# Loading half of batch 0's values in rows, and multiplying g into the tokens instead of the weights

## The chip, the cores and the metric

The kernel runs on one core of a Trainium2 chip. The core has five instruction queues that run side by side and wait for each other through semaphores: TensorE (PE, matrix products and turns), VectorE (DVE), ScalarE (ACT), GpSimd (POOL) and SyncE (SP). POOL and SP also issue the transfers between the chip's main memory and the core's on-chip memory. The metric is the device time of one launch in microseconds, less is better.

## The reference, cut to what matters

Two blocks follow each other. The first is attention in chunks: 4 batches, 8 heads, 768 positions, 64 values per head. Each chunk of 32 queries sees 8 memory keys, 16 keys to its left, its own 32 and 8 to its right, 64 in all.

```python
for c in range(nc):
    l_start = max(0, c_start - left_ctx)
    r_end = min(S, c_end + right_ctx)
    k_full = np.concatenate([mem_k, k[:, :, l_start:r_end]], axis=2)
    v_full = np.concatenate([mem_v, v[:, :, l_start:r_end]], axis=2)
    scores = scale * np.matmul(q_c, k_full.transpose(0, 1, 3, 2))
    a = np.exp(scores - scores.max(-1))
    a = a / (a.sum(-1) + 1e-09)
    out[:, :, c_start:c_end] = np.matmul(a, v_full)
```

The second is a normalisation and a two-layer network over the 512 features of each position, added to its input:

```python
xn = (x - mu) / np.sqrt(var + 1e-06) * g_ln
ch = np.maximum(xn @ w_ch1, 0.0) @ w_ch2
return x + ch
```

The vector `g_ln` has one factor per feature. It can be multiplied into the tokens `x - mu` or, since it runs along the rows of `w_ch1`, into that matrix. The division by the root is the same for a whole token and positive, so the kernel does it last, on the result of the second product.

## The kernel before, in words

The tokens are worked in 24 tiles of 128 positions, six to a batch. Tile t goes through these steps:

- `qk(t)`: 64 small products of queries and keys into PSUM (L316), the row maximum (`row_max`, L325, DVE), the difference (`less_max`, L328, DVE) and the exponential (`weights`, L338, ACT).
- `pt(t)`: four turns of the weights on PE (L348) and a copy.
- `val(t)`: 32 small products with the values `V` (L362), then `tokens` on DVE (sum of weights, quotient, mean; L371 to L378), and `shift`, which takes the mean off and rounds to 16 bits (`xn`; L385 on POOL, L389 on ACT).
- `turn_x(t)`: four turns on PE (L414) and a copy into `xT` (L420).
- `root(t)`: the variance on ACT (L400) and two small POOL instructions for `rstd` (L404, L408).

Two tiles are a unit u, twelve in all. `up(u, s)` for s from 0 to 7 is the first layer (L452) with its relu (L443 or L445). The second layer is `down(0, part)` (L477) for unit 0 and `down7(u, part)` (L528) for the others: seven products of blocks, from sums of the relu's results (`r_sum`, L522) and of w2's blocks (`w2_sum`, L507).

The keys and queries come in as octets of rows (`load_octets`, L111, two transfers a call) and are turned on PE into streams with blocks of 72 columns. For batches 1 to 3 two heads are first interleaved by a copy (`mix`, L246), so that one turn (L255) does the work of two (L214).

The values lie in `V[b % 2]`, 128 rows for each of 12 groups of 64 positions: the memory's rows, the rows that a group's two chunks share, and the rest. In batch 0 all values go the way of the keys: octets, turns (`turn_v`) into the stream `VT`, then per group eight turns (`v_products`, L285) and a copy into `V` (`v_copy`, L296). From batch 1 on they are loaded by head straight into rows (`load_v_head`, L120 and L125, and `load_v_ends`, L131 and L135, all issued on POOL in pieces of 64 values); the shared rows are copied inside the chip by `v_shared` (L142) and the memory's by `v_mem` (L147), both issued on SP.

The order of the work is written out by hand: straight code for units 0 and 1 (L603 to L819), then a plan of calls by unit and step (L821 to L904). Every engine runs its own part of that order and never overtakes. That holds for the issue of transfers too: a load on POOL stands in line with POOL's fills and small sums, a copy on SP in line with the stores of finished tokens. In the straight code PE is also given products of zeros (`warm`, L599) where it would have nothing to do.

In the code before, POOL multiplies g into the four quarters of w1 (`scale_w1`, L434, 16 calls) after their loads: the first two quarters before the loads of w1's third and fourth, the last two after the loads of w2.

## Time and profile before

| what | value |
|---|---|
| time, median of 3 runs (lowest, highest) | 231.99 us (231.17, 232.43) |
| the profiled execution: its time, its span | 231.75 us, 230.0 us |
| PE, DVE, ACT, POOL busy | 95%, 70%, 54%, 50% of the span |
| w2's last quarter lands | 38.23 us |
| POOL's last load of batch 1's values: issue ends, lands | 60.83 us, 62.34 us |
| `val(2)`, `val(4)`, `val(6)` start on PE | 32.92, 46.18, 69.19 us |
| up(2, 0), the first product of unit 2, starts on PE | 59.34 us |

The profile is of one execution. Its times count from the start of the span; 1.75 us of the execution's time lie around the span. PE's busy time holds the products of zeros too, so a busy PE in the first 20 us is not all useful work. A page has the busy times, the span in 40 slices, the chain of work that ended last and the costliest groups; further views list the instructions of an engine in order of time (start, duration, line, what was written and read, how often; in brackets the idle time before it and what ended it), and the busy times by stretches. The trace also has the time at which most transfers landed.

### The profile page before, as it was taken

Reading aid. Unit: us, or ns where it says so; the run is one execution under the profiler, and the core shown is the slowest. Engines: PE = TensorE matmul, PEld = TensorE weight load, DVE = VectorE, ACT = ScalarE, POOL = GpSimd, SP = SyncE. Lnnn points to the kernel's source line nnn. Section 1 sums busy time; section 2 is a strip of 40 time slices with the busy share of each in tenths; the row PEclk is TensorE's granted clock in tenths of the full one; section 3 lists DMA queues with packets and bytes.
Section 4 is the critical chain, followed back from the end, with each engine's and each line's share of the span. In section 5 each row is a group of like instructions: output and inputs, shape, how many; then the busy total and the mean of one; then the engine's idle time right before and its main releaser. Section 6 shows DMA issues by size and latency. Waiting matters only on the chain.

```text
span 230.0 us, 8554 instructions
## 1 busy us (share of the span) xinstructions
PE 218.4 (95%) x3720; PEld 190.0 (83%) x3720; DVE 162.1 (70%) x380; ACT 124.6 (54%) x237; POOL 115.4 (50%) x197
## 2 busy tenths in 40 slices
PE   7979787999999989999999999999999999999993
PEld 3546675886898979989989999999999999899982
DVE  3576654678998996796587796894784875646372
ACT  2244475888552748649645468478447265343310
POOL 7889897589965594913724946513031121220000
PEclk9999999999999999999999999999999999999999
DMA  5999999998999899963881992942102002011022
GB/s 79 188 205 205 214 215 200 187 77 55 61 155 152 149 90 111 138 87 42 149 115 51 119 154 56 106 91 67 48 3 91 3 3 91 3 48 46 1 94 93
DMA packets 43282, 23.25 MB, mean 101 GB/s; under 512 B 29884, under 2 KB 39676, under 8 KB 43172
## 3 DMA queue, kind: packets, MB, share of 16 engines
q0 software_dynamic: 38320, 14.48, 52.9%
q1 hardware_dynamic: 4924, 8.22, 12.8%
q8 instruction: 29, 0.48, 0.8%
q14 instruction: 9, 0.07, 0.1%
HBM read 29.02 MB, written 6.29 MB: 153 GB/s over the span
## 4 chain that ended last, share of the span: by engine, by line
PE 86%; DVE 6%; issue 3%; ACT 2%; POOL 1%; DVEq 0%; POOLq 0%
PE upb L452 34%; PE dnb L528 28%; PE two L362 4%; PE one L255 3%; PE dnb L477 3%; PE one L316 3%; PE one L414 2%; PE two L599 2%; PE one L348 2%; POOL raw L111 1%; DVE sub L328 1%; DVE xs L372 1%; DVE KT L227 1%; DVE nmx L325 1%; ACT rT L443 1%
## 5 line engine op out<-in xcount | busy, mean ns | idle before, releaser
L452 PE MATMUL upb<-xT,w1c 128*128 128x256 f16 x736 | 94.9, 273 | 1.6 <-issue 1.4
L452 PEld LDWEIGHTS <-w1c 128*128 128x128 f16 x736 | 77.8, 114 | 3.6 <-issue 1.5
L443 ACT ACTIVATE rT<-upb 128x512 f16<-128x512 f32 x92 | 53.5, 594 | 37.8 <-PE upb L452 34.9
L535 DVE SCALAR_TENSOR_TENSOR xs<-dnb,rstd,xs 128x256 f32<-128x256 f32 x77 | 37.0, 481 | 27.2 <-PE dnb L528 26.3
L528 PEld LDWEIGHTS <-RS 128*128 128x128 f16 x352 | 33.8, 98 | 3.7 <-issue 0.2
L338 ACT ACTIVATE P<-sub 128x512 f16<-128x512 f32 x24 | 15.2, 634 | 37.1 <-DVE sub L328 36.8
L528 PE MATMUL dnb<-T,RS 128*128 128x256 f16 x264 | 33.9, 273 | 0.0
L385 POOL TENSOR_SCALAR xn<-xs,nmean 128x512 f16<-128x512 f32 x18 | 12.7, 707 | 35.6 <-PE upb L452 20.6
L404 POOL TENSOR_SCALAR veps<-ssq 128x1 f32<-128x1 f32 x24 | 4.9, 204 | 45.9 <-ACT sq L400 45.6
L528 PEld LDWEIGHTS <-rT 128*128 128x128 f16 x264 | 25.2, 98 | 2.5
L528 PE MATMUL dnb<-w2c,rT 128*128 128x256 f16 x176 | 22.7, 272 | 0.0
L522 DVE TENSOR_TENSOR RS<-rT 128x1024 f16<-128x1024 f16 (+2 forms) x23 | 15.2, 663 | 8.9 <-ACT rT L443 8.9
L120 POOL DMA_DIRECT2D V<-in_v_dram x24 | 20.9, 871 | 1.2 <-PE dnb L528 0.7
L400 ACT ACTIVATE sq<-xs,nmean 128x512 f16<-128x512 f32 x24 | 17.3, 721 | 0.1
L372 DVE CUSTOM_DVE_ANT_1 xs<-two,rec 128x512 f32<-128x512 f32 x24 | 16.6, 691 | 0.8
L325 DVE TENSOR_REDUCE nmx<-one 128x8 f32<-128x512 f32 x22 | 15.1, 685 | 1.2 <-PE one L316 1.2
L408 POOL TENSOR_TENSOR rstd<-veps,mhalf 128x1 f32<-128x1 f32 x24 | 14.9, 621 | 2.0
L328 DVE TENSOR_TENSOR sub<-one,nmx 128x512 f32<-128x512 f32 x22 | 15.2, 692 | 0.8
L125 POOL DMA_DIRECT2D V<-in_v_dram x24 | 15.5, 647 | 0.0
L353 ACT COPY PT<-one 128x512 f16<-128x512 f16 x21 | 12.2, 586 | 5.6 <-PE one L348 5.6
L255 PEld LDWEIGHTS <-raw 96*128 96x128 f16 x192 | 10.6, 97 | 2.0 <-issue 0.8
L420 DVE COPY xT<-one 128x512 f16<-128x512 f16 x21 | 8.8, 420 | 4.5 <-PE one L414 4.1
(115 smaller groups left out, 312.2 us busy)
## 6 DMA issues: line engine op xcount, KB each, us to landing
out_dram<-xs SPq DMA_DIRECT2D x23, 256.0 KB, 2.5
raw<-in_k_dram POOLq DMA_DIRECT2D x16, 192.0 KB, 5.8
raw<-in_q_dram POOLq DMA_DIRECT2D x12, 192.0 KB, 6.3
w1c<-in_moe_w_ch_dram POOLq DMA_DIRECT2D x4, 512.0 KB, 8.8
w2c<-in_moe_w_ch_dram POOLq DMA_DIRECT2D x4, 512.0 KB, 12.5
V<-in_v_dram POOLq DMA_DIRECT2D x24, 77.0 KB, 3.7
V<-V SPq DMA_DIRECT2D x3, 360.0 KB
V<-in_v_dram POOLq DMA_DIRECT2D x24, 44.0 KB, 3.4
```

What stands on the lines that cost most here:

```text
L120: nc.gpsimd.dma_start(out=V[b % 2][72:128, 0 : NG - 1, h, 0:64], in_=dram(v, base + 16 * D, [[64, 56], [64 * 64, NG - 1], [1, 64]]),)
L125: nc.gpsimd.dma_start(out=V[b % 2][0:32, 1:NG, h, 0:64], in_=dram(v, base + 48 * D, [[64, 32], [64 * 64, NG - 1], [1, 64]]),)
L255: nc.tensor.matmul(out=pv[:, 96 * r : 96 * r + 96], lhsT=mixed[i][0:96, jj, r, :], rhs=identity[0:96, 0:96], is_transpose=True, start=True ...
L325: nc.vector.tensor_reduce(out=nmx[t % 2], in_=scores, axis=AX.X, op=ALU.max)
L328: nc.vector.tensor_tensor(out=sub[t % 2].rearrange("p (c k) -> p c k", c=8), in0=scores, in1=free(nmx[t % 2], 0, [[1, 8], [0, 64]]), op=AL ...
L338: nc.scalar.activation(out=P[t % 3], in_=sub[t % 2], func=ACTF.Exp, scale=0.125)
L372: nc.vector.tensor_tensor_reduce(out=x.rearrange("p (h d) -> p h d", h=H), in0=free(two, 0, [[128, 8], [1, 64]]), in1=free(r, 0, [[1, 8], ...
L400: nc.scalar.activation(out=sq, in_=xs[t % 9], func=ACTF.Square, bias=nmean[t % 6], scale=1.0, accum_out=ssq[i],)
L443: nc.scalar.activation(out=o, in_=i, func=ACTF.Relu)
L452: nc.tensor.matmul(out=p[:, 256 * hb : 256 * hb + 256], lhsT=free(w1c[hc // 4][:, dt, :], hc % 4, [[4, 128]]), rhs=xT[u % 3][:, dt, :], st ...
L528: nc.tensor.matmul(out=p[:, 0:256], lhsT=left[:, n, :], rhs=right(n), start=(n == 0 and not add), stop=(n == 7), skip_group_check=add,)
L535: nc.vector.scalar_tensor_tensor(out=x, in0=p[:, 0:256], scalar=rstd[t % 9], in1=x, op0=ALU.mult, op1=ALU.add,)
```

## The change

Five things are changed, all but one of them in the straight code for units 0 and 1.

1. The second half of batch 0's values is no longer loaded as octets and turned. A new function loads a group of `V` in rows, in two transfers, and groups 5 to 11 come that way, spread between the loads of w1 and w2 on POOL. Their memory rows and shared rows come by `v_mem(0, 5)` and `v_shared` on SP. Groups 0 to 4 are made as before.
2. `scale_w1` is gone. g is loaded as a row repeated on all 128 partitions (`g_row`), and `shift` multiplies it into the tokens: on DVE in one instruction for tiles 0 to 5 (they were on ACT), on POOL in two for the other 18 tiles (it was one).
3. The second keys and queries of batch 0 are interleaved like those of later batches: the keys by two copies on POOL, the queries by two on ACT, and then turned in half as many matmuls.
4. The two turns of the memory's keys and values are joined into one, and the memory rows of all batches are loaded at once and earlier.
5. The order of the code at the start is written anew. The fills of `V[1]` (`ready_v`) keep their place on POOL, between the first and the second loads of batch 1's keys and queries; ahead of them now stand all row groups. Some relus, copies and products of zeros change engine or number; 99 tiny products of zeros replace seven large ones at the very start.

```diff
+    def load_v_group(b, g):
+        lo = b * H * HS + 64 * g * D
+        rows = 56 if g < NG - 1 else 48
+        nc.gpsimd.dma_start(
+            out=V[b % 2][72 : 72 + rows, g, :, 0:64],
+            in_=dram(v, lo + 16 * D, [[64, rows], [HS, H], [1, 64]]),
+        )
+        nc.gpsimd.dma_start(
+            out=V[b % 2][0:32, g, :, 0:64],
+            in_=dram(v, lo - 16 * D, [[64, 32], [HS, H], [1, 64]]),
+        )
...
             nc.gpsimd.tensor_scalar(
-                out=xn[i], in0=x, scalar1=nmean[t % 6], scalar2=1.0, op0=ALU.add, op1=ALU.mult,
+                out=xc, in0=x, scalar1=nmean[t % 6], scalar2=1.0, op0=ALU.add, op1=ALU.mult,
             )
+            nc.gpsimd.tensor_tensor(out=xn[i], in0=xc, in1=g_row, op=ALU.mult)
         else:
-            nc.scalar.activation(
-                out=xn[i], in_=x, func=ACTF.Identity, bias=nmean[t % 6], scale=1.0,
+            nc.vector.scalar_tensor_tensor(
+                out=xn[i], in0=x, scalar=nmean[t % 6], in1=g_row, op0=ALU.add, op1=ALU.mult,
             )
...
+    nc.sync.dma_start(out=g_row, in_=dram(moe_g_ln, 0, [[0, 128], [1, 512]]))
...
     load_w1(0)
-    load_w1(1)
     load_octets(0, 1, k, 0, 48, 48)
     load_octets(1, 1, q, 0, 32, 64)
-    load_octets(2, 1, v, 0, 48, 48)
+    load_w1(1)
+    load_mem_rows(0, B)
+    load_w1(2)
+    mix(0, 1, "P", 1)
...
+    mix(1, 1, "A", 0, 128)
...
+    last_k(0, "A")
+    last_k(1, "A")
+    load_v_group(0, 5)
+    load_w1(3)
+    for g in (6, 7):
+        load_v_group(0, g)
+    v_mem(0, 5)
+    v_shared(0, 5, 8)
...
+    for c in range(2):
+        load_w2(c)
+    for g in (8, 9):
+        load_v_group(0, g)
     for c in range(2, 4):
         load_w2(c)
...
+    for g in (10, 11):
+        load_v_group(0, g)
+    v_shared(0, 8, NG)
...
-    for c in range(2, 4):
-        for dt in range(4):
-            scale_w1(c, dt, "P")
     load_octets(0, 0, k, 1, 0, 48)
     load_octets(1, 0, q, 1, 0, 48)
-    load_mem_rows(1, B)
     ready_v(1, nc.gpsimd)
     v_mem(1)
...
-    v_turn(5, "V")
...
-    val(2, "A")
+    val(2, "V")
...
     load_octets(0, 1, k, 1, 48, 48)
     load_octets(1, 1, q, 1, 48, 48)
...
-    up(1, 5, "V")
+    up(1, 5, "A")
```

## The prediction

> **What bounds the kernel now.** I read the page first: PE is busy 95% of the span, and in the 40 slices it is short of full only in the first eight. The chain that ended last says the same: 86% PE, most of it the two big products (L452, L528). So after about 45 us every microsecond is PE work in a fixed order, and a change can win or lose time only by when PE gets through the start, or by a new wait later.
>
> Next the table by stretches (engine busy times, then granted clock, DMA share, GB/s) and the page's DMA rows:
>
> ```profile
> PE   7979787999999989999999999999999999999993
> DMA  5999999998999899963881992942102002011022
> 20.00:25.00 5.00, 4.78 (x137) 3.81 (x134) 3.02 (x7) 2.59 (x4) 4.05 (x8) 1.00 1.24 206
> ...
> 35.00:40.00 5.00, 3.57 (x96) 2.73 (x94) 2.01 (x7) 2.59 (x5) 3.74 (x7) 1.00 1.19 201
> 50.00:55.00 5.00, 5.00 (x83) 3.14 (x81) 4.37 (x15) 3.81 (x9) 4.76 (x8) 1.00 0.63 42
> ```
>
> The DMA share stays above 1 (packets overlap) from 5 to 45 us: the POOL queue's transfers land one after another without a gap. It falls to 0.63 only after 50 us. So a transfer added at the start moves all that follow it.
>
> Then the order of time on POOL, on SP's queue and on PE:
>
> ```profile
> 38.78 1.14 POOL L111 DMA_DIRECT2D raw<-in_q_dram  x2 [0.83 <-DMA w2c<-in_moe_w_ch_dram]
> 40.24 0.84 POOL L120 DMA_DIRECT2D V<-in_v_dram  x1 [0.32 <-DMA raw<-in_k_dram]
> ...
> 60.26 0.57 POOL L135 DMA_DIRECT2D V<-in_v_dram  x1
> 62.31 0.79 SPq L142 DMA_DIRECT2D V<-V  x1
> 46.18 0.42 PE L362 MATMUL two<-V,PT 64*32 64x65 f16 x32
> 69.19 0.42 PE L362 MATMUL two<-V,PT 64*32 64x65 f16 x32
> ```
>
> A load on POOL waits until the eighth load before it has landed: the one at 38.78 waits for w2's last quarter, which the trace lets land at 38.23. POOL then issues all of batch 1's values, its last load at 60.26 to 60.83, landing at 62.34. Only then can SP start the copy of the shared rows (62.31), whose packets end at 67.86. The first use of those values is `val(6)` on PE at 69.19. So this chain has only 69.19 - 67.86 = 1.3 us to spare.
>
> **The change part by part.** The profiled execution took 231.75 us (span 230.0, 1.75 around it), 0.24 below the median 231.99; sums are made on 231.75.
>
> *PE, ACT, DVE at the start.* PE loses seven `v_turn` (38.85 to 39.20: 0.35 each, 2.45), two value turns (28.64 to 29.44: 0.8), half of four k/q turns (8 matmuls on L255 take 0.34 where 16 on L214 take 0.5 to 0.64: about 0.9) and one of two mem turns (half of 0.86): 4.6 us. DVE and ACT lose seven copies into V (0.41 or 0.60 each). ACT is instead held by `mix(1, 1, "A")` behind q's second half (now landing near 18), so `PT(1)` is copied about 2 us later than its 18.23; the relu of `up(1, 5)` and `up(1, 7)` (0.69 each) goes from DVE to ACT, while DVE takes the shift of tokens 0 to 5 (nearest rows 0.69 for a subtract, 0.80 for L484, against ACT's 0.72). I cost all of this at nothing: it lies ahead of `val(4)`, where the next item ends last. That cover is about five microseconds thick: from `val(2)` to `val(4)` PE had 46.18 - 32.92 = 13.3 us with 1.6 of idling and 1.4 of `v_turn` in it; with val(2) near 32, PE would now be at `val(4)` near 42.
>
> *POOL before 40 us.* It loses 16 scalings of w1 (0.68 each, 10.9 us) and two octet loads (1.2); it gains two `mix` copies 96x1024 (between 0.98, a memset of 128x1024, and 2.3, by 0.289 for 32x128 on L693; I take 1.37, two scalings' worth, the like-sized read and write), 14 row loads (0.6 to 0.7 each by the 384-row and 128-row L131, L135) and as many more slots in the wait of eight. All of it is issued ahead of the full queue, so it costs nothing there.
>
> *The transfers.* Ahead of w2's last quarter the queue loses v's second half (20.65 to 22.40 in landings: 1.75) and gains five row groups of 448 + 256 pieces. Price of a piece: V's first two loads, 616 each, landed 1.38 us after the queue's load before them (46.08 to 47.46), so 1.12 ns and 0.79 us a group. Low bound 0.83 ns (352 + 616 + 616 landing between 50.35 and 51.67), 0.59 us; high bound 1.56 ns (1936 pieces from 58.36 to 61.38, paced by POOL's issue), 1.10 us. I take 0.79, the row with the fullest queue: 3.95. The mem rows come earlier (192 pieces added 0.15 at 42.10: 0.2). g as 128 rows, 256 KB, on SP's queue beside the first k (whose second load landed at 6.64): 0.4, between 0 and 0.8 (by one 256 KB tile at 204 KB/us being 1.3, less g's old 512 small pieces). SP's copies of mem and shared rows, some 230 KB at 204 KB/us, 1.1 at most, 0 if they fit between; I take 0.7. Sum: -1.75 + 3.95 + 0.2 + 0.4 + 0.7 = +3.5, between +1.4 and +5.9. w2's last quarter lands at 41.7. The Trainium skill, DMA: Bandwidth & Descriptors, "Anatomy of one DMA", gives the moving part as bytes / 436 GB/s, 0.41 us for a group's 180 KB read; by it the sum here would be +1.6 and the time some 1.9 lower. The 1.12 ns row is the measurement, and it stands.
>
> Behind this, `val(4)` needs the copy of groups 8 to 11, which waits for group 11 (43.0): with the 1.75 us that SP's copy needed from issue to first packet (62.31 to 64.06) and about 1.3 of packets, 46.1. It was at 46.18. So PE gains nothing by then, and 23.0 us of unbroken PE work (46.18 to 69.19) follow as before.
>
> *POOL behind w2.* The second half of q for batch 1 (first set) now waits for w2's last quarter, 0.28 after it (as at 10.80 after 10.52): 42.0. From there POOL has no free time: that load 0.57, the four fills of V[1] (33.47 to 36.57: 3.1, which before lay ahead of the wait and now lie behind it), four octet loads 2.3, eight L120 7.2, eight L125 5.3, the ends 1.2, four `root` pairs 3.9: 23.6. Last issue ends at 65.6 instead of 60.83: +4.8. Before, POOL had 2.8 us of waits for ACT in this stretch; they are eaten up.
>
> *The new wait.* Less the 1.3 us to spare, `val(6)` waits until 72.7: +3.5, between +1.4 and +5.9. Behind it on PE stands everything that is left; SP's stores of tokens 0 and 1 stand behind the copy, their buffers being needed only by `val(9)` (86.42).
>
> *g in the shift.* From token 6 on POOL does a second pass per tile, 18 times. Its price is not in the trace: at least one one-input pass (0.69, L385), at most two (1.38); I take 1.0, since it reads two tiles and writes one. Time between shift and turn in before: token 6 1.02, 7 1.19, 8 0.53, 9 1.83, 22 1.54, the others 1.7 and more. Token 6 just holds. Token 7 is hit twice, since POOL puts two q loads (1.15) between the shifts: 71.63 + 1.0 + 1.15 + 0.05 + 0.69 + 1.0 = 75.5 against a turn at 75.08, 0.4. Token 8, where POOL works without a gap from 79.71: 86.52 + 1.0 - 87.05 = 0.5. Later ones are covered by the 1.5 to 2.8. Sum +0.9 (0.3 to 2.0). The row says 0.69 for one input; the Trainium skill, GPSIMD Engine Reference, "Elementwise — side-by-side cycle accounting", gives 2.6 cycles an element at 1.2 GHz for two inputs, 1.1 us here, by which this item would be 1.2. No run here shows it yet.
>
> Together 231.75 + 3.5 + 0.9 = 236.15, so **236.1 us, slower by 1.9%**. Its own range, from 1.4 + 0.3 to 5.9 + 2.0, is 233.4 to 239.6.
>
> **The rivals.** *Faster: the row groups fill holes.* If the five groups, g and SP's copies add nothing to the queue, w2's last quarter lands at 36.5, POOL's last issue ends at 36.8 + 23.6 = 60.4 and V[1] is ready at 67.4; `val(4)` is released near 41, PE reaches `val(6)` before 67.4, 1.7 less than 69.19. With the cheap second pass: 231.75 - 1.7 + 0.3 = 230.3. For: POOL lags behind the queue nowhere, and PE's 4.6 us are real. Against: a share above 1 for 40 us. It decides once all additions together stay below some 0.5 us.
>
> *Nearly even: the wait is just covered.* With every addition at its low end (+1.4), and POOL's 23.6 us of issues some 1.2 us quicker, `val(6)` moves by 0.2 and, with 0.3 to 0.9 for the shift, the time is 232.2 to 232.9. Against: POOL's loads in 53 to 61 us ran without a wait and were no quicker.
>
> *Slower by another place: the second pass is dear.* If it takes 2.5 us, all turns of odd tokens from 9 on are late by 0.7 to 0.8 (slack 1.7), eight of them 6 us, beside the wait for V[1]: 240 or more. Nothing in the trace speaks for so much.
>
> **How the numbers follow.** Main case 0.57; dear second pass or another slower cause 0.14; nearly even 0.09; faster 0.20. The time can be told from no change at about 0.5%. Slower 0.71, same 0.09, faster 0.20. The low end 230.3 is the faster rival's own time and leaves out what lies beyond it, about 0.1; the high end 239.6 is the main case's upper bound and leaves out the dear pass beyond it.
>
> **What would show it.** Right: DMA share above 1 until past 50 us; w2's last quarter landing near 41.7; PE idle before L362's successor (`val`) near 42 to 46 and again near 69 to 73, the latter ended by SP's copy; POOL without a gap from 42 to 66; one turn of tokens 7 and 8 waiting for POOL. Wrong: V[1]'s last load landing before 64, a `val(6)` that does not wait, or row groups landing in 0.5 us each.

## The result, and the profile after

The changed kernel takes 241.36 us, the median of four runs (240.01 to 242.22). Before, measured beside it, takes 232.21 us (231.17 to 232.94). The ratio is 1.039, with a 95% interval from 1.032 to 1.046: the change costs about 9 us, where the terms of the forecast added up to 4.4. Runs that lie over 1.5% above the fastest of their kernel are left out of medians, ranges and ratios below. The profiled execution of after took 242.22 us with a span of 240.5; before's span was 230.0. All places below count from the start of a span, so 10.5 us have to be found; the profiled execution is the slowest of its four, and the medians differ by 9.2. Executions of a kernel can differ by a few us here, and places by as much as 1.5: in the profiles of four kernels whose code is the same up to `val(6)` (after twice, and two experiments below that change only POOL's second pass), w2's last quarter lands at 41.28 to 42.10 and `val(6)` starts at 72.67 to 74.14. So medians and ratios decide, and places are used where they differ by more than that or lie close together in one trace.

From the page of after, PE, the granted clock and DMA in 40 slices of 6 us, then the chain that ended last by engine:

```profile
PE   6687849999986697999999999999999999999993
PEclk9999985999999999999999999999999999999999
DMA  4999999999999959595294396962201102011022
...
PE 51%; DMA 14%; DVE 11%; POOL 11%; ACT 7%; issue 6%; POOLq 0%; ACTq 0%; SPq 0%; DVEq 0%
```

Before, PE was full from the eighth slice on, but for an 8 in the fifteenth. Now it has a second hole in the 12th to 14th slices, 66 to 84 us, and a smaller one in the 16th, 90 to 96. The chain that ended last was 86% PE; now DMA, DVE, POOL and "issue" have large shares. The table by stretches (busy time of PE, of its weight load, of DVE, ACT and POOL with counts, then granted clock, DMA share, GB/s) shows the holes in the start and at `val(6)`, and the transfers that now come later:

```profile
34.00:38.00 4.00, 1.90 (x39) 1.59 (x40) 1.14 (x5) 0.59 (x1) 1.64 (x3) 0.61 1.35 213
38.00:42.00 4.00, 4.00 (x82) 2.75 (x81) 2.91 (x7) 0.60 (x1) 1.86 (x4) 0.54 1.41 183
...
50.00:55.00 5.00, 5.00 (x77) 3.46 (x75) 3.30 (x12) 4.16 (x12) 4.16 (x8) 1.00 1.23 145
69.00:74.00 5.00, 2.07 (x22) 1.71 (x19) 2.42 (x5) 2.93 (x6) 3.60 (x6) 1.00 0.86 143
```

The DMA share from 50 to 55 us is 1.23; it was 0.63. The order of time on POOL, then on SP's queue, then on PE, gives the chain behind that:

```profile
42.39 0.58 POOL L110 DMA_DIRECT2D raw<-in_q_dram  x1 [1.77 <-DMA w2c<-in_moe_w_ch_dram]
42.95 1.40 POOL L579 MEMSET V<- 128x1536 f16 x1
...
55.01 0.84 POOL L119 DMA_DIRECT2D V<-in_v_dram  x1 [0.41 <-DMA raw<-in_k_dram]
...
57.70 1.36 POOL L124 DMA_DIRECT2D V<-in_v_dram  x2 [0.69 <-issue]
...
66.74 0.53 POOL L147 DMA_DIRECT2D V<-in_v_dram  x1
68.56 0.78 SPq L154 DMA_DIRECT2D V<-V  x1
36.10 0.62 PE L370 MATMUL two<-V,PT 64*32 64x65 f16 x30 [3.27 <-DMA V<-V]
...
74.14 0.42 PE L370 MATMUL two<-V,PT 64*32 64x65 f16 x32 [3.08 <-DMA V<-V]
```

w2's last quarter landed at 42.10 (38.23 before). The q load that waits for it goes out at 42.39, the fills of `V[1]` come behind it, POOL's last value load is issued by 67.27 (60.83), the copy of the shared rows on SP at 68.56 (62.31), and `val(6)` starts at 74.14 instead of 69.19. PE would have been there at 71.06 and stands still for 3.08 us.

Where the span's 10.47 us (242.22 - 231.75) went, by PE's starts of the same step in both traces (worked out from the two orders of time on PE):

| place | us |
|---|---|
| `val(6)` starts later: 74.14 - 69.19 | 4.95 |
| turn of token 6 | 0.38 |
| a stop of PE behind `val(7)`, 78.95 to 80.84, "issue" | 2.06 |
| turn of token 8, which waits for POOL's second pass | 0.92 |
| turns of tokens 10, 11, 16 and 17 (0.40, 0.38, 0.51, 0.27) | 1.56 |
| the end, and what is below 0.2 each | 0.60 |

So 4.95 us are lost by `val(6)` and 5.52 behind it. The second sum is the surprise. The groups of after that bear on it (busy us, mean ns of one, then idle time before them and what ended it):

```profile
L396 POOL TENSOR_TENSOR xn<-xc,g_row 128x512 f16<-128x512 f32 x18 | 23.3, 1293 | 1.5
L393 POOL TENSOR_SCALAR xc<-xs,nmean 128x512 f32<-128x512 f32 x18 | 12.9, 717 | 33.9 <-PE upb L445 20.1 <-DVE nmean L386 13.6
L515 DVE TENSOR_TENSOR RS<-rT,RS 128x1024 f16<-128x1024 f16 x11 | 11.5, 1043 | 0.0
```

and the same two places in before:

```profile
L385 POOL TENSOR_SCALAR xn<-xs,nmean 128x512 f16<-128x512 f32 x18 | 12.7, 707 | 35.6 <-PE upb L452 20.6 <-DVE nmean L378 14.5 <-PE one L414 0.4
L522 DVE TENSOR_TENSOR RS<-rT,RS 128x1024 f16<-128x1024 f16 x11 | 7.5, 681 | 0.0
```

POOL's second pass takes 1293 ns. And one of the sums on VectorE, which the change does not touch, went from 681 to 1043 ns on average. It is not slower everywhere: five of the eleven take 1.45 to 1.47 us, one 0.75, the others 0.68 as before. Those five start while POOL's second pass runs. In the sixth meeting the sum starts first, at 143.17; it takes 0.75, and POOL's pass, begun at 143.46, takes 1.59. In the order of time of after, one such meeting on DVE, POOL and PE:

```profile
109.32 0.69 DVE L336 TENSOR_TENSOR sub<-one,nmx 128x512 f32<-128x512 f32 x1
109.92 1.45 DVE L515 TENSOR_TENSOR RS<-rT,RS 128x1024 f16<-128x1024 f16 x1
111.30 0.47 DVE L528 SCALAR_TENSOR_TENSOR xs<-dnb,rstd,xs 128x256 f32<-128x256 f32 x1
111.70 1.01 DVE L238 COPY KT<-one 128x192 f16<-128x192 f16 x2
109.55 1.28 POOL L396 TENSOR_TENSOR xn<-xc,g_row 128x512 f16<-128x512 f32 x1
112.75 0.38 PE L423 MATMUL one<-identity,xn 128*128 128x128 f16 x4 [0.33 <-DVE KT L238]
```

POOL's pass runs from 109.55 to 110.83. The sum starts at 109.92 and ends at 111.38, 0.55 after the pass. The subtraction just ahead of it, which reads PSUM, runs beside the same pass and keeps its 0.69. What follows on DVE is 0.78 late, and the turn of token 10 on PE waits for it.

The trace of before has one such meeting, the other way round, on DVE and POOL:

```profile
197.37 0.68 DVE L522 TENSOR_TENSOR RS<-rT,RS 128x1024 f16<-128x1024 f16 x1
197.62 0.98 POOL L385 TENSOR_SCALAR xn<-xs,nmean 128x512 f16<-128x512 f32 x1 [6.77 <-DVE nmean L378]
```

There POOL's one pass begins 0.25 into the sum, takes 0.98 where such a pass takes 0.69 elsewhere, and ends 0.56 after the sum. So in all these meetings the operation that starts second ends some 0.5 us or more after the first, and the sign of it stood in the trace that the forecast was made from.

### The profile page after: what moved, and what is told of

It is laid out like the page before. It is cut to its first block, busy times and chain, and to the rows that moved or that the text cites. A ratio compares the mean times of both kernels' runs of the same rounds, so it can differ in the third digit from the quotient of the medians.

```text
span 240.5 us, 8427 instructions
## 1 busy us (share of the span) xinstructions
PE 217.5 (90%) x3654; PEld 189.0 (79%) x3654; DVE 164.7 (68%) x372; ACT 123.6 (51%) x234; POOL 137.7 (57%) x213
## 4 chain that ended last, share of the span: by engine, by line
PE 51%; DMA 14%; DVE 11%; POOL 11%; ACT 7%; issue 6%; POOLq 0%; ACTq 0%; SPq 0%; DVEq 0%
PE upb L445 21%; PE dnb L521 18%; DMA raw<-in_k_dram 8%; DMA V<-in_v_dram 3%; PE dnb L470 3%; DMA V<-V 2%; ACT rT L436 2%; POOL V L119 2%; PE two L370 2%; DVE RS L515 2%; DVE xs L528 2%; PE one L423 2%; DVE sub L336 2%; DVE nmx L333 2%; ACT sq L409 2%
## 5 line engine op out<-in xcount | busy, mean ns | idle before, releaser
L445 PE MATMUL upb<-xT,w1c 128*128 128x256 f16 x752 | 98.4, 276 | 2.5 <-issue 1.9
L445 PEld LDWEIGHTS <-w1c 128*128 128x128 f16 x752 | 80.3, 115 | 5.3 <-issue 2.7
L436 ACT ACTIVATE rT<-upb 128x512 f16<-128x512 f32 x96 | 56.0, 596 | 42.9 <-PE upb L445 42.9
L346 ACT ACTIVATE P<-sub 128x512 f16<-128x512 f32 x24 | 15.2, 632 | 41.7 <-DVE sub L336 41.7
L393 POOL TENSOR_SCALAR xc<-xs,nmean 128x512 f32<-128x512 f32 x18 | 12.9, 717 | 33.9 <-PE upb L445 20.1
L396 POOL TENSOR_TENSOR xn<-xc,g_row 128x512 f16<-128x512 f32 x18 | 23.3, 1293 | 1.5
L370 PEld LDWEIGHTS <-PT 64*32 64x32 f16 x768 | 7.9, 95 | 13.5 <-issue 11.4
L370 PE MATMUL two<-V,PT 64*32 64x65 f16 x768 | 11.0, 195 | 8.0 <-DMA V<-V 6.4
L361 ACT COPY PT<-one 128x512 f16<-128x512 f16 x21 | 12.1, 584 | 6.8 <-PE one L356 6.8
L417 POOL TENSOR_TENSOR rstd<-veps,mhalf 128x1 f32<-128x1 f32 x24 | 14.1, 586 | 2.0
L379 DVE RECIPROCAL rec<-two 128x8 f32<-128x8 f32 x24 | 4.8, 200 | 14.1 <-PE two L370 13.9
```

The costliest lines, as they stand in the source:

```text
L346: nc.scalar.activation(out=P[t % 3], in_=sub[t % 2], func=ACTF.Exp, scale=0.125)
L370: nc.tensor.matmul(out=two[col : col + 32, 128 * h : 128 * h + 65], lhsT=PT[t % 3][rows, 2 * (h // 4) + h % 2, q0 : q0 + 32], rhs=V[b % 2] ...
L396: nc.gpsimd.tensor_tensor(out=xn[i], in0=xc, in1=g_row, op=ALU.mult)
L436: nc.scalar.activation(out=o, in_=i, func=ACTF.Relu)
L445: nc.tensor.matmul(out=p[:, 256 * hb : 256 * hb + 256], lhsT=free(w1c[hc // 4][:, dt, :], hc % 4, [[4, 128]]), rhs=xT[u % 3][:, dt, :], st ...
```

## The experiments

The ratios are to the kernel before on the same chip, whose medians were 231.7 to 232.4 us. "Stretch" is the time from the start of `val(6)` to the end of the span: 160.85 in before, 166.37 in after. PE's work in it is the same in all kernels.

### Is it g, or the loads?

The change in two halves: g multiplied into the tokens alone, on top of before; and the whole change with g as a column factor instead, multiplied in when a turned token is copied, so without the repeated row and without a second pass.

```diff
 (g into the tokens alone: before, with)
-    nc.sync.dma_start(out=g_col, in_=dram(moe_g_ln, 0, [[1, 128], [128, 4]]))
+    nc.sync.dma_start(out=g_row, in_=dram(moe_g_ln, 0, [[0, 128], [1, 512]]))
-            scale_w1(c, dt, "P")
...
+            nc.gpsimd.tensor_tensor(out=xn[i], in0=xc, in1=g_row, op=ALU.mult)
```

> The kernel before with part 2 of the change alone: g out of w1, into the tokens by the same instructions as in the changed kernel, values loaded as before. Theories 1 and 2 together: the first keys land 2.4 us late, but some of it is lost in the waits of the start, so val(6) moves from 69.2 to 70 to 71.6; behind it the second pass adds 2.9; time 236 to 237.5. Rival (the row groups are the cause of nearly all): val(6) at 69.2 or earlier since POOL is rid of 16 scalings, time 232 to 233.

```diff
 (g as a column: after, with)
-            nc.gpsimd.tensor_tensor(out=xn[i], in0=xc, in1=g_row, op=ALU.mult)
...
-        nc.vector.tensor_copy(
+        nc.vector.tensor_tensor(
...
-            in_=pv.rearrange("p (d c) -> p d c", d=4),
+            in0=pv.rearrange("p (d c) -> p d c", d=4),
+            in1=free(g_col, 0, [[1, 4], [0, 128]]), op=ALU.mult,
...
-    nc.sync.dma_start(out=g_row, in_=dram(moe_g_ln, 0, [[0, 128], [1, 512]]))
+    nc.sync.dma_start(out=g_col, in_=dram(moe_g_ln, 0, [[1, 128], [128, 4]]))
```

> The changed kernel with g multiplied in as a column of 512 factors in the copy behind the tokens' turn on DVE (features stand on partitions there), so without g's repeated row, without DVE's product in the shift and without POOL's second pass; all else of the change stays. Theory (g's two costs are 2.4 us of the transfer queue and 3 to 4 us behind val(6); the rest is row loads and order): first keys land near 6.7, w2's last quarter near 39.7, val(6) near 71.7, the stretch behind it 161 to 162, time 234.5. Rival (the row loads and the new order cost nearly all that val(6) lost): val(6) near 73.5, time 236.5.

| kernel | median us (range) | ratio to before | `val(6)` | stretch |
|---|---|---|---|---|
| g into the tokens alone | 238.63 (237.58 to 238.70) | 1.025 [1.017, 1.033] | 71.97 | 164.89 |
| the rest, g as a column | 238.07 (235.90 to 238.43) | 1.025 [1.020, 1.030] | 72.93 | 161.26 |
| all of it (after) | 241.36 | 1.039 [1.032, 1.046] | 74.14 | 166.37 |

The groups of "g into the tokens alone" have the slow sum too, with none of the new loads:

```profile
L389 POOL TENSOR_TENSOR xn<-xc,g_row 128x512 f16<-128x512 f32 x18 | 23.5, 1304 | 1.5
L508 DVE TENSOR_TENSOR RS<-rT,RS 128x1024 f16<-128x1024 f16 x11 | 11.4, 1034 | 0.0
```

(The column's profile is of its fastest execution, 235.90 us.) So g in the tokens costs 6.4 us by itself, 4.0 of its profile's span behind `val(6)`. The rest costs 5.7 by itself, and in its profile 3.7 of 4.1 us lie ahead of `val(6)`. The two add up to 12.1 and not to the 9.2 of all of it. Both delay `val(6)`, g alone by 2.8, and if only the later delay counts there, the 2.9 too many are accounted for; no run tests that by itself.

The column was then put on before alone, with the scalings of w1 taken out, to see whether a cheap way to bring in g wins what the scalings cost:

```diff
-            scale_w1(c, dt, "P")
...
+        nc.vector.tensor_tensor(
...
+            in1=free(g_col, 0, [[1, 4], [0, 128]]), op=ALU.mult,
```

> The kernel before with g as a column in the copy behind the turn, and no scaling of w1: what moving g to the tokens is worth without the repeated row and the second pass. POOL loses 10.9 us of scalings, which lay beside a full queue; DVE gains 24 times 0.28 us. Theory: val(6) within 0.5 us of 69.2, the stretch behind it 160.9 to 161.5, time 231.5 to 233, no difference that can be told. Rival (POOL's scalings did hold the start): val(6) 1 us or more earlier, time 230.5 to 231.

232.55 us (231.99 to 233.23, ten runs), ratio 1.0001 [0.9975, 1.0027]. No difference: taking 10.9 us of scalings off POOL gains nothing. `val(6)` was at 70.11, 0.9 later than in before, where at most 0.5 was expected, and w2's last quarter landed at 38.75 (38.23), so the queue was no faster either.

### What the second pass on POOL costs, and how

One pass for tokens 6 to 23, and then two passes of which the second has one input only:

```diff
 (one pass)
-                out=xc, in0=x, scalar1=nmean[t % 6], scalar2=1.0, op0=ALU.add, op1=ALU.mult,
+                out=xn[i], in0=x, scalar1=nmean[t % 6], scalar2=1.0, op0=ALU.add, op1=ALU.mult,
-            nc.gpsimd.tensor_tensor(out=xn[i], in0=xc, in1=g_row, op=ALU.mult)
 (second pass with one input)
-            nc.gpsimd.tensor_tensor(out=xn[i], in0=xc, in1=g_row, op=ALU.mult)
+            nc.gpsimd.tensor_scalar(
+                out=xn[i], in0=xc, scalar1=1.0, scalar2=1.0, op0=ALU.mult, op1=ALU.mult,
+            )
```

> The changed kernel, with POOL's shift in one pass for tokens 6 to 23 (it leaves g out of those tokens). Theory 2 (the second pass costs 2.9 us behind val(6): turns of tokens 6 and 8 late by 1.3, and DVE's sums held up while POOL's two-input pass runs, 1.6): val(6) stays at 74.1, the stretch from val(6) to the end goes from 166.4 to about 163.4, time 238.4; DVE's sums of relu results are back at 0.68 everywhere. If the idle time of 1.9 us in PE at 79 hangs on it too, 161.3 and 236.4. Rival (the prediction's 0.9): 165.5, time 240.5.

> The changed kernel with POOL's second pass as a pass of one input (times 1.0; it leaves g out of tokens 6 to 23): two passes of 0.7 us in place of 0.7 and 1.29. Theory (DVE's sum of two tiles is held while a POOL instruction is at work on the same memory, whatever its number of inputs; it is the time on POOL that counts): where the second pass meets DVE's sum, the sum is again longer than 0.68, by up to 0.2 to 0.7, and the stretch behind val(6) lies between 162.1 and 166.4. Rival (only a POOL instruction of two inputs holds DVE): all sums at 0.68 and the stretch within 0.7 of 162.1.

| kernel | us (range) | ratio | stretch |
|---|---|---|---|
| after | 241.36 | 1.039 [1.032, 1.046] | 166.37 |
| one pass | 236.70 (236.49 to 239.88) | 1.022 [1.011, 1.032] | 162.11 |
| second pass with one input | 239.25 (one run) | | 164.36 |

The groups of the kernel with one pass:

```profile
L514 DVE TENSOR_TENSOR RS<-rT,RS 128x1024 f16<-128x1024 f16 x11 | 7.5, 682 | 0.0
```

and of the one whose second pass has one input:

```profile
L396 POOL TENSOR_SCALAR xn<-xc 128x512 f16<-128x512 f32 x18 | 11.6, 646 | 1.5
L517 DVE TENSOR_TENSOR RS<-rT,RS 128x1024 f16<-128x1024 f16 x11 | 8.0, 730 | 0.0
```

Without the second pass no sum is slow, and the stretch is 4.3 us shorter. Of these, 1.2 are PE's stop behind `val(7)`, which takes 0.70 here and 1.90 in after. (`val(6)` is at 72.67, where 74.1 was expected: nothing ahead of it was changed, so this is the spread between executions.) With a short second pass of one input, five sums take 0.78 to 0.80: less, but each of them ends 0.54 us after POOL's pass ends, as with two inputs (0.55). So it is not POOL's two inputs that count. The sum is held until POOL's pass is over, and a longer pass holds it longer. (Of this run's stretch, 1.6 us are between `val(6)` and `val(7)`, where the clock was low after a stop, and 0.9 are PE's stop behind `val(7)`. Less these it is 161.9, and one pass less its own stop is 161.4, so the sums show the hold and the stretch of this run does not price it.)

### g's row at the start

The repeated row's load, 256 KB, moved from SP's queue to POOL's behind w1's first quarter; and, in its old place, 128 different rows of the same size.

```diff
 (row behind w1's first quarter)
-    nc.sync.dma_start(out=g_row, in_=dram(moe_g_ln, 0, [[0, 128], [1, 512]]))
...
+    nc.gpsimd.dma_start(out=g_row, in_=dram(moe_g_ln, 0, [[0, 128], [1, 512]]))
 (different rows)
-    nc.sync.dma_start(out=g_row, in_=dram(moe_g_ln, 0, [[0, 128], [1, 512]]))
+    nc.sync.dma_start(out=g_row, in_=dram(moe_w_ch1, 0, [[FF, 128], [1, 512]]))
```

> The changed kernel with one edit: g's repeated row is loaded on POOL's queue behind w1's first quarter instead of on SP's queue beside the first keys. Theory 1 (the repeated row, not the row groups, made the first keys land 2.4 us late, and the lateness is handed down the full queue to batch 1's values): the first keys' second load lands near 6.7 instead of 9.07, w2's last quarter near 39.7 instead of 42.1, val(6) starts near 71.8 instead of 74.1, time about 239. Rival (the queue pays the same 2.4 us wherever the row stands): the keys are early, but w2's last quarter still lands at 42, val(6) at 74, time 241.4.

> The changed kernel, with g's tile loaded from 128 different rows of w1 instead of one row 128 times: the same bytes and pieces on the same queue, other numbers in place of g. If it is the volume that delays the first keys, they still land near 9.0. If it is that all 128 pieces read the same 2 KB, they land near 6.8 to 7.2, as 256 KB at the queue's rate would have it.

| kernel | us | first k complete | w2's last quarter | `val(6)` |
|---|---|---|---|---|
| before | 232.2 | 6.64 | 38.23 | 69.19 |
| after | 241.36 | 9.07 | 42.10 | 74.14 |
| row behind w1's first quarter | 241.4 (240.34 to 242.14), 1.038 [1.030, 1.045] | 6.58 | 42.70 | 74.62 |
| different rows | 241.53 (one run) | 8.44 | 41.75 | 73.81 |
| g as a column | 238.07 | 7.38 | 41.01 | 72.93 |

The rival held for the first: the first keys come 2.5 us earlier and nothing is won, as the queue pays elsewhere. With different rows the first keys are complete 0.6 earlier than in after, but the same repeated row gives 8.65 to 9.30 in the four profiles named above, so little or nothing of the 2.4 us is due to the repetition and most to the volume. Against the column, the row costs w2's last quarter 1.1 us in this pair, and 0.3 to 1.1 over the 41.28 to 42.10 of those profiles.

### The fills, and the low clock

The fills of `V[1]` ahead of w2's loads, so ahead of the wait; then that with 14 zero products ahead of `val(2)`, so that PE does not stop there; and the memory rows of batch 1 (`v_mem(1)`) ahead of w2's loads, on the version with the copies split by groups that is described below.

```diff
 (fills early)
+    ready_v(1, nc.gpsimd)
...
-    ready_v(1, nc.gpsimd)
 (and warm)
+    warm(14, upb[0])
 (memory rows early, on another version)
+    v_mem(1)
...
-    v_mem(1)
```

> The changed kernel with the four fills of V[1] moved on POOL ahead of the first loads of w2, where POOL waits for landings anyway. Theory 3 (POOL's unbroken chain behind w2's last quarter decides when batch 1's values are there): POOL's last value load is issued some 3 us earlier, at about 64, val(6) starts when PE comes to it, about 71.1, time 238.3. Rival (the queue of transfers itself decides, POOL only fills it): the values land within 1 us of the 68.8 of the changed kernel, val(6) at 73 to 74, time 240.5 to 241.4.

> The kernel with the fills of V[1] ahead of w2, and 14 products of zeros on PE (3 us) ahead of val(2), where PE stood idle for 2.8 us from 33.4 and the granted clock then showed 0.50 from 38 to 44. Theory 4 (the idle time itself brings the low clock, and the low clock costs some 2 us up to val(4)): the clock stays at 1.00 from 34 to 44, val(2) takes its values at the same 36, val(4) starts at 46.5 to 47.3 instead of 49.05; val(6) still waits for its values, 72 to 72.5, and the time stays near 239. Rival (val(4) is late for the values of groups 8 to 11 anyway): val(4) stays within 0.5 us of 49.

> The kernel with g as a column, early fills and split copies, and SP's copies of the memory rows for batch 1 moved ahead of w2's loads (they ran from 48 to 54 beside the second keys and queries of batch 1, whose four loads then took 8.5 us to land instead of 4). If that collision is the next link: those loads land by 52 instead of 55.7, batch 1's values by 63, val(6) starts at 68 to 69, time 231 to 232.5. If the queue only pays it earlier: w2's last quarter lands 2 us or more later, val(6) stays at 71, time 234 to 235.5.

With the fills early: 239.63 us (239.37 to 241.49), 1.032 [1.024, 1.039]. From its order of time, POOL's last value load and `val(6)`:

```profile
64.42 0.56 POOL L147 DMA_DIRECT2D V<-in_v_dram  x1
72.53 0.42 PE L370 MATMUL two<-V,PT 64*32 64x65 f16 x32 [0.45 <-ACT PT L361]
```

POOL's last issue ends 2.3 us earlier and `val(6)` no longer waits for V. It gains only 1.7 in the medians, which the two intervals do not tell apart, since PE itself comes late: it left `val(4)` at 49.05, and 23 us of work lie between. So there are two delays, one behind the other: PE's own start, and V.

With the zero products (239.2 us, one run) the clock stays at 1.00 from 34 to 48 us, where it was 0.50 from 38 to 44 without them. `val(4)` is at 49.22 all the same, as it waits for the copy of the row groups. So the low clock cost nothing there.

The memory rows early: 236.5 us (235.46 to 238.72), 1.015 [1.012, 1.019], against 234.8 and 235.5 in the two runs of its base: no gain. w2's last quarter lands at 43.88 instead of 41.43, and `val(6)` is at 71.64. The rival held: the queue only pays earlier.

### The row groups

Batch 0's groups 5 to 11 not loaded at all, and the values zero. In the first of the two runs the zeros were filled in on VectorE, in the second on POOL.

```diff
-        nc.gpsimd.dma_start(
-            out=V[b % 2][72 : 72 + rows, g, :, 0:64],
...
+        return
...
 (first run)
+    nc.vector.memset(V[0][:, 5:NG, :, 0:64], 0.0)
 (second run)
+    nc.gpsimd.memset(V[0][:, 5:NG, :, :], 1.0)
```

> The changed kernel without the 14 transfers of the row groups: the values of groups 5 to 11 of batch 0 stay zero, so it leaves that part of the loads out. What stays is g's row, the second pass, the order. If the groups cost the queue what their landings in the changed kernel say (0.4 to 0.5 us each, five ahead of w2's last quarter): that lands at 39.5 to 40.2 instead of 42.1, val(6) starts at 71.5 to 72, time 239. If they cost the prediction's 0.79 each: 38.2, val(6) at 70, time 237.5. If they cost nothing: 42.1 and 74.1.

> The changed kernel without the loads of batch 0's row groups 5 to 11 (those values are zeros, filled in on POOL near the start, where the run with the fill on VectorE held the first keys; so the outputs of batch 0 are not the reference's). Theory (the loads that stand ahead of w2's last quarter on the common transfer engines set val(6), through POOL's queue): w2's last quarter lands near 39.4 (42.1 in the changed kernel), POOL's last value load is issued by 64.7 (67.3), val(6) starts near 71.6 (74.1), and what is left of the delay, some 2.4 us against the kernel before, belongs to g's row and to the second k and q loads that run beside v_mem(1). Rival (val(6) hangs on the copy of the shared rows and its own queue, whatever the groups): val(6) stays within 0.5 us of 74.1.

(The second run's fill holds ones, not the zeros that its expectation names; no time hangs on that.) The first run, 244.06 us, tells little: the fill held VectorE, and PE stopped for 7.4 us at 17.9. It shows only w2's last quarter at 39.38. The second: 237.91 us (one run). Its order of time on POOL, SP and PE:

```profile
40.02 0.58 POOL L110 DMA_DIRECT2D raw<-in_q_dram  x1 [2.71 <-DMA w2c<-in_moe_w_ch_dram]
...
59.32 0.53 POOL L138 DMA_DIRECT2D V<-in_v_dram  x1
62.70 0.78 SPq L145 DMA_DIRECT2D V<-V  x1
68.19 0.42 PE L361 MATMUL two<-V,PT 64*32 64x65 f16 x32
```

`val(6)` at 68.19 does not wait. That is 5.95 us earlier than after, and 1.0 earlier than before: more than either theory gave. w2's last quarter lands only 2.4 us earlier (39.73). But POOL's last issue is 7.4 earlier (59.85), because without 14 row loads in the line the wait for w2's last quarter falls on a later load: the fills (3.15 us) and three of the second k and q loads (1.7) now stand ahead of it. 2.4 + 3.15 + 1.7 is nearly all of it. Of the 5.95 us the time keeps only 3.5: the stretch behind `val(6)` is 168.0, 1.6 longer than in after, as PE's stop behind `val(7)` takes 2.64 us and the clock is 0.50 for 3.4 us after it.

### The last link: the copy of the shared rows

Three versions with g as a column and the fills early. In the first, the shared-row copies of batch 0 are split by groups (5, 6 to 7, 8 to 9, 10 to 11); it was run twice. In the second, batch 1's shared rows are also copied by heads, 0 to 5 as soon as these are there and 6 to 7 at the end. In the third, all loads that fill shared rows go first and the copy is again one. Places of the first version are those of its second run.

```diff
 (split by groups)
-    v_shared(0, 5, 8)
+    v_shared(0, 5, 6)
+    v_shared(0, 6, 8)
...
 (by heads, on top)
+    load_v_ends(1)
...
-    load_v_ends(1)
...
-    v_shared(1, 0, NG)
+    v_shared_heads(1, 0, 6)
+    v_shared_heads(1, 6, 8)
 (shared rows first, on top of by heads)
-        load_v_head(1, h, 1)
+    for h in range(6, 8):
+        load_v_head(1, h, 0)
...
-    v_shared_heads(1, 0, 6)
-    v_shared_heads(1, 6, 8)
+    v_shared(1, 0, NG)
```

> The former run's kernel, with the fills of V[1] ahead of w2's first loads on POOL, and the copies of shared rows in batch 0 split in four, so that each starts when its groups have landed. If POOL's chain and the two late copies are what holds PE: val(2) runs through without the stop of about 3 us, val(4) comes at 45 to 46, batch 1's values land near 62 to 64, val(6) starts at 68 to 69, time 230.5 to 232. If the queue of transfers itself is the bound, val(6) stays near 71.5 and the time near 234.

> The version with g as a column, the early fills and the copies split, and in it batch 1's end rows loaded before the eight groups and the copy of the shared rows split by heads (0 to 5, then 6 and 7) instead of by groups, so that the larger part goes before the last load. Theory (V's second half is the last link ahead of val(6), and 1.5 to 3 us of it are the copy behind the last load): val(6) starts at 69.5 to 70 (71.31), the time is 232.5 to 234. Rival (the queue and the second k and q loads set it, the copy only follows): val(6) within 0.5 us of 71.3 and the time 235 to 236.5.

> The version with the copy split by heads, but with the loads that fill the shared rows of heads 6 and 7 ahead of the second-part loads of heads 4 and 5, and the copy again in one piece, as it now waits for no late load. Theory (the last link ahead of val(6) is the copy behind the loads of the shared rows): the copy is issued near 62 to 63, its packets end by 67, the wait of 1.3 us at val(6) goes, and the time is 230.6 to 231.5, some 0.5% below the kernel before. Rival (the copy runs beside the last four loads and is slowed by them, or these loads, landing near 68.6, become the last link): val(6) stays at 68 to 68.6 and the time at 231.5 to 232.5.

> The version with g as a column, the early fills and the copy of the shared rows split by groups, once more: its first profile was of an execution at the upper end of its times, so the places in it say little. Theory (the copy behind the last loads is the last link ahead of val(6)): val(6) still waits for it by 2 us or more and starts at 70.5 to 71.5; median 234 to 235.5. Rival (what the copy by heads won was an accident of the executions): val(6) at 68.5 to 69.5 and a median within 1 us of the copy by heads.

| kernel | median us (range) | ratio to before | `val(4)` | `val(6)`, of it a wait | stretch |
|---|---|---|---|---|---|
| split by groups | 234.75 (232.84 to 236.26) | 1.010 [1.002, 1.018] | | | |
| the same again | 235.46 (235.26 to 235.86) | 1.016 [1.012, 1.020] | 43.98 | 69.76, 2.54 | 163.97 |
| copy by heads | 231.87 (230.88 to 233.24) | 0.998 [0.994, 1.001] | 44.13 | 68.47, 1.12 + 0.17 | 161.71 |
| shared rows first | 232.16 (230.94 to 234.04) | 1.002 [0.999, 1.006] | 44.42 | 68.79, 1.15 | 162.83 |

The copy split by groups (the second of the two runs), on SP's queue and on PE:

```profile
64.54 0.78 SPq L153 DMA_DIRECT2D V<-V  x1
69.76 0.63 PE L369 MATMUL two<-V,PT 64*32 64x65 f16 x32 [2.54 <-DMA V<-V]
```

The copy by heads:

```profile
62.92 3.43 SPq L157 DMA_DIRECT2D V<-V  x2
68.47 0.36 PE L373 MATMUL two<-V,PT 64*32 64x65 f16 x24 [1.12 <-DMA V<-V]
69.01 0.24 PE L373 MATMUL two<-V,PT 64*32 64x65 f16 x8 [0.17 <-DMA V<-V]
```

The last link is the copy: from its issue to the release of `val(6)` it takes 5.2 us (64.54 to 69.76), in after 5.6 (68.56 to 74.14). The split by groups was expected at 230.5 to 232 and missed that in both runs. By heads, the second part goes out at 65.56 and PE is free at 69.01, 3.45 later. In the third version the copy goes out at 63.33, its loads have all landed by 65.08, and still `val(6)` starts at 68.79: a whole copy beside the last loads needs 5.5 us, so the rival held. Between the profiles of the split by groups and of the copy by heads lie 3.6 us: 1.3 at `val(6)`, 1.1 from there to `val(7)` with the low clock, and 1.2 in PE's stop behind `val(7)` (1.75 and 0.55). The copy by heads is as fast as before and no faster. None of these versions beats it measurably.

### The changed kernel once more

> The changed kernel once more, to see which of its gaps repeat. Theory: val(6) starts at 74.1 +- 0.5, five sums of VectorE take 1.4 to 1.5 us, and the stretch behind val(6) is 166.4 +- 0.6 with the TensorE stop of 0.9 to 2.0 us between 77 and 81 behind the 16 KB transfer of the instruction queue. Rival: the stop is an accident of one execution; without it the stretch is 164.3 to 164.6.

241.67 us. `val(6)` at 73.94, stretch 166.0, the same five sums at 1.45 to 1.47. The stop repeats too, as PE's order of time shows:

```profile
78.45 0.30 PE L445 MATMUL upb<-xT,w1c 128*128 128x256 f16 x1
80.57 0.95 PE L445 MATMUL upb<-xT,w1c 128*128 128x256 f16 x7 [1.82 <-issue]
```

It lasted 1.90, 1.82 and 1.77 us in three executions of after's code (one with different rows for g). Each time a 16 KB transfer of the instruction queue had begun 0.5 to 0.7 us before it (78.36, 78.08, 78.12) and took 0.9.

It is not tied to g: of the 16 profiles of after's code and of versions made from it, 13 have the stop, of 0.55 to 3.27 us. It stands at one place of PE's order, the 1243rd to 1245th product of the trace. With the 14 zero products ahead of `val(2)` it comes 14 products earlier in the work, in the middle of the score products:

```profile
76.34 0.32 PE L324 MATMUL one<-KT,QD 64*32 64x64 f16 x19
77.60 0.29 PE L324 MATMUL one<-KT,QD 64*32 64x64 f16 x13 [0.94 <-issue]
```

In all 13, PE goes on 2.3 to 2.9 us after the 16 KB transfer began. In the three without a stop (row behind w1's first quarter, g as a column, the first run of the split by groups) PE comes to that place 3.1 to 3.7 us after it began. So the stop is a wait at a fixed place of PE's instruction stream that ends a fixed time after that transfer, as a wait for the instructions in it would. No run changed the transfer itself, and what sets its start is open.

## Why the prediction was wrong, point by point

The direction and the first mechanism were right: `val(6)` became a wait for `V[1]`, ended by SP's copy, behind POOL's chain that starts at w2's last quarter. The size was wrong. 236.1 was forecast with a range to 239.6, and 241.36 was measured. By the profile, 10.5 us came where 4.4 were forecast: 1.5 more in the wait for V, 2.6 more through g in the shift (3.5 in place of 0.9), and 2.1 in a stop of PE that is in no term.

**PE, ACT and DVE at the start, costed at nothing.** The cover was partly gone. `val(2)` was forecast near 32 without a stop; it started at 32.62 and stopped 3.27 us for the copy of groups 5 to 7, and `val(4)` came at 47.84, not 46.1. With V in time, PE would have reached `val(6)` at 71.06, so this alone would have cost 1.9 us. It lies under the wait for V and added nothing to it; the run with early fills, where V is in time, meets it.

**The transfers, +3.5.** w2's last quarter landed at 42.10; 41.7 was forecast. But the terms were off and made up for each other. The groups cost 2.4 us (39.73 without them), not 3.95: 0.47 each, where the row of 0.79 was taken. Groups 8 and 9 land 0.47 us each in after's own trace too (36.07 to 37.01 for both). g's row cost 0.3 to 1.1 where 0.4 was put, and delayed the first keys by 2.4. The rest is some 2 to 3 us that no run splits, where 0.9 was put for memory rows and SP's copies. That these errors nearly cancelled was luck. For the price of a group the estimate of 0.41 us worked out from the Trainium skill, DMA: Bandwidth & Descriptors, "Anatomy of one DMA", was nearer to the measured 0.47 than the row that was kept.

**POOL behind w2, 23.6 us.** The q load went out at 42.39 (forecast 42.0) and the last issue ended at 67.27 (65.6): 24.9 us. The 1.3 us more are mostly two gaps that the forecast ruled out with "POOL has no free time": 0.41 for a load of k, and 0.69 before 57.70, for which the profile names no releaser. The run without groups bears out the core of this step: what pushed POOL was less the landing (2.4) than that the fills and three loads fell behind the wait (4.85).

**The new wait, +3.5.** Measured +4.95, which is the two terms above: 0.4 from the queue and 1.3 from POOL, less 0.2 in the copy. One pass, with the same code ahead of `val(6)`, had it at 72.67, just the forecast 72.7, so this term lies within the spread of executions.

**g in the shift, +0.9: the step that failed.** With g alone on before, where PE's stop behind `val(7)` is absent, it cost 4.0 us behind `val(6)` (164.89 against 160.85). In after it cost 4.3 to 5.1 by the two other pairs (one pass 162.11, column 161.26, against 166.37), and 3.1 to 3.2 once the stop is taken off each (1.90 in after, 0.70 with one pass, none with the column). Three things were missing in the forecast.

- The pass takes 1.29 us, not 1.0, near the upper of its bounds, 0.69 and 1.38. The Trainium skill, GPSIMD Engine Reference, "Elementwise — side-by-side cycle accounting", from which an estimate of 1.1 was worked out, is below the measurement as well. With g alone the turns of tokens 6, 7 and 8 are late by 0.4, 0.8 and 0.9, where 0, 0.4 and 0.5 were forecast. In after they are 0.38, nothing and 0.92, as the stop ahead of token 7's turn hides its part; that their sum came near the forecast's 0.9 there was luck.
- VectorE's sums of two 16-bit tiles wait while POOL's pass runs: 0.78 each, five times, and through them four turns, 1.56 us. The forecast priced the second pass only by the slack of the turn that waits for it, "later ones are covered by the 1.5 to 2.8", and did not ask whom POOL's pass holds. The Trainium skill has a rule that speaks against this change and was not weighed: SBUF — State Buffer, "SBUF: two separate sides", says that VectorE and GpSimd share a pair of ports as an exclusive lock, held for the whole instruction, and that a VectorE operation with two SBUF inputs takes part in it against a GpSimd operation that reads SBUF. The trace agrees: 1.45 against 0.68 us, the sums end 0.55 after POOL's pass, and the subtraction from PSUM beside it keeps its 0.69.
- PE's stop of 1.9 us near 79. It is in no term of the forecast, and it is there in versions without the second pass too (1.75 us with the copies split by groups, 2.10 with the shared rows first, 3.27 with the memory rows early), so it does not come from g, though its length shifts with the timing of each version.

**The rivals.** The faster one, that groups fill holes, is out: the queue stayed full. "Nearly even" is out. "The second pass is dear" ended nearest in size, but not by its mechanism: it took the pass at 2.5 us, and the measured 1.29 did the damage through VectorE.

**What would show it.** The DMA share past 50 us (1.23, though 0.77 from 46 to 50), w2's last quarter near 41.7, and PE idle at `val(6)` ended by SP's copy came true. "PE idle near `val(4)`" came at `val(2)`, and POOL had two small gaps. The late turns were those of tokens 6 and 8. One of the signs of being wrong came true as well: row groups landed in 0.47 us each. None of the signs named looked at VectorE, where the unforecast part could have been seen.

## What to carry to other kernels

Price a new pass on POOL by what it holds as well as by its own time: put each two-input operation of VectorE that reads on-chip memory beside it, and take for each meeting the end of the one that starts first as the earliest end of the other. A load added to a queue that is full, where each load waits for the eighth before it (the loads here take eight semaphores in turn), costs its own transfer and also moves the whole line behind the wait; the second was twice the first here. And two delays ahead of one step do not add, so take them away one at a time before believing a sum.

## What the runs showed of the hardware that was not expected

- A two-input sum on VectorE (128x1024, 16 bits, 0.68 us) was held to 1.45 to 1.47 us by POOL's 1.28 us pass, and to 0.78 to 0.80 by one of 0.61; in both it ended 0.54 to 0.55 after POOL's pass. Where the sum started first, POOL's pass was held: 1.59 in place of 1.28 us (after, 143.46), 0.98 in place of 0.69 (before, 197.62).
- The copy of the shared rows inside the chip (24 rows of 15 KB read and written, on SP's queue) took 5.2 to 5.6 us from its issue to the release of PE in three kernels, beside other transfers.
- After a stop of PE the granted clock was 0.50 in some executions and 1.00 in others: 0.50 after stops of 3.33 us (row behind w1's first quarter), 2.54 (split by groups, again) and 2.04 (second pass with one input), with 3.7 to 4.1 us from `val(6)` to `val(7)` instead of 2.21; 1.00 after 3.08 (after) and 2.45 (memory rows early). The clock records of the traces show when: a granted clock holds for whole multiples of 3.41 us, so it changes on a fixed grid. What counts is how much of one such window PE was idle, not how long the stop was. Over all profiles, from 30 us on, all 14 windows at full clock with 2.04 us or more of idle time were followed by 0.50, and none with 1.81 or less. The stop of 2.04 lay in one window; that of 3.08 was cut by a boundary into 1.35 and 1.73. The Trainium skill, TensorE: Matmul & The Clock Gate, "Part 1: The HAM clock gate (the "warmup" mystery)", gives an idle window of some 3.4 us that runs freely. The traces agree with the length and the free running, and show besides that the window need not be idle throughout: 2.04 of 3.41 us were enough.
- PE stopped for 0.55 to 3.27 us at one fixed place of its instruction stream in 13 profiles, and each time went on 2.3 to 2.9 us after a 16 KB transfer of the instruction queue had begun.
